# Four kv heads in one 128-partition tile, with a block mask on the attention weights, in a decode attention kernel

## The chip, the cores and the metric

The kernel runs on one core of one Trainium2 chip. The metric is device time in microseconds (us) of one execution. The span in a profile is a little shorter than the time (205.2 us against 207.02 us in the profiled run of the kernel before). Each run is therefore marked fast, slow or, where it stands alone, unknown, and only fast runs are compared.

Engine names in the profile: PE is TensorE (matmuls), PEld its weight loads, DVE is VectorE, ACT is ScalarE, POOL is GpSimd, SP is SyncE, which issues the DMAs here.

## The reference, cut to what matters

```python
# B=8 sequences, one new token each; D=512; 32 query heads, 8 kv heads, head size 128; cache of 8192
def _A_ref(x, k_cache, v_cache, wq, wo):
    W = min(4096, max(256, Sk // 4))                  # 2048: only the last 2048 positions count
    q = (x @ wq).reshape(B, 1, 32, 128) ...
    k = jnp.repeat(k_cache[:, :, Sk - W:, :], 4, axis=1)
    v = jnp.repeat(v_cache[:, :, Sk - W:, :], 4, axis=1)
    p = softmax(einsum("bhqd,bhkd->bhqk", q, k) * 128 ** -0.5)
    return einsum("bhqk,bhkd->bhqd", p, v) ... @ wo

h  = x + _A_ref(layernorm(x), k_cache, v_cache, wq, wo)
out = h + _B_ref(layernorm(h), ...)                   # a small MLP, not touched by the change
```

All data are bfloat16. The caches are 8 sequences x 8 heads x 2048 positions x 128 values, 33.6 MB each for K and V, and every byte is used once. With one token per sequence there is little arithmetic per byte. The natural limit is the rate at which K and V come in (408 GB/s in the profile below).

A word on correctness: with the given inputs attention moves the output very little, so that the comparison with the reference passes even for a kernel whose attention is wrong.

## The kernel before: the parts that matter

A step is one kv head of one sequence, 2048 positions. Its K lies in SBUF as 128 partitions of 16 positions, which is one run of 4 KB per partition in HBM. Sixteen 128x128 transposes turn it into `kT` (head size on partitions, positions along the free axis). Four QK matmuls, one per quarter of the positions, go to four column groups of the array. The query operand `qblk[:, b, g, :]` is zero outside the heads of kv head `g`, so the eight steps of a sequence accumulate into one 128 x 512 score tile in PSUM, whose partitions are 4 quarters x 32 query heads.

```python
e.dma_start(knat[:, ks, :].rearrange("p (c d) -> p c d", c=NC),          # NC = 16: 4 KB per partition
            A_k_cache[b, g, W0:SK, :].rearrange("(p c) d -> p c d", c=NC)).then_inc(sem_k[ks], 16)
...
def pe_T(e, i):                                  # 16 transposes of one step
    ...
    for c in range(NC):
        ins = e.matmul(buf[:, c * 128:(c + 1) * 128], knat[:, ks, c * DH:(c + 1) * DH],
                       ident_b[:, :], is_transpose=True)
...
def pe_QK(e, i):                                 # 4 matmuls of 512 neighbouring columns
    ...
    for q in range(4):
        ins = e.matmul(S_ps[32 * q:32 * (q + 1), b % 2, :], qblk[:, b, g, :],
                       kT_sb[:, i % NKT, 512 * q:512 * (q + 1)],
                       start=(g == 0), stop=(g == G - 1), tile_position=(0, 32 * q), ...)
...
def act_exp(e, b):                               # one exp per sequence, 512 neighbouring values written
    ...
    e.activation(P_sb[:, j, :], S_ps[:, j, :], ACT.Exp, bias=negmcol[:, j:j + 1], scale=1.0,
                 accum_out=lcol[:, j:j + 1]).then_inc(sem_exp, 1)
...
def pe_PT_lrowT(e, b):                           # 4 transposes of P
    ...
def pe_PV(e, b, glist, first, last):             # 128 matmuls of 4 columns per sequence
    ...
            e.matmul(misc[:, ...], vnat[:, vs, c * DH:(c + 1) * DH], pT_sb[:, b % 2, c, R * g:R * (g + 1)], ...)
```

The order of work on TensorE is one software pipeline: the transposes of step p, QK of step p-2, and in the steps after a sequence's last QK its max, exp, P transposes and PV. K has 15 slots of 512 KB, V has 16.

## Time and profile before

| | before |
|---|---|
| time, median of 3 runs | 207.6 us (207.4 to 207.75) |
| span of the profiled run, mean granted clock | 205.2 us, 0.834 |
| busy TensorE / ScalarE / VectorE | 159.2 / 81.4 / 83.5 us |
| DMA rate between 20 and 160 us | 408 GB/s |
| TensorE waiting for K ahead of its transposes | 20.8 us, 22 times |

The first lines are the page's view of the span in 40 slices. Each digit is a tenth of the slice: busy share for PE and DMA, granted clock for PEclk.

```profile
PE   1039975999599967995799878797998698875745
PEclk9999999797979799979995998599859797675557
DMA  6999999999999999999999999999999999999980
GB/s 206 434 398 415 409 407 409 407 411 408 403 410 406 408 410 410 406 406 410 409 410 405 409 411 410 407 406 410 406 409 408 407 410 385 359 394 328 394 334 28
```

DMA is full from the second slice almost to the end, at 403 to 415 GB/s while the caches stream. TensorE has holes, and its clock drops now and then (to about 0.5 in the lowest slices). The chain that ended last, by engine and by line, says the same: 84% of the span hangs on DMA and on the queue that issues it.

```profile
DMA 53%; SPq 31%; PE 13%; issue 2%; DVE 0%
...
```

Then the groups of instructions (line, engine, operation, out<-in, shapes, count | busy us, mean ns | idle before, and what ended most of it):

```profile
L388 PE MATMUL kT_ps<-ident_b,knat 128*128 128x128 bf16 x1024 | 83.8, 248 | 21.7 <-DMA knat<-in_A_k_cache_dram 20.8
L418 PE MATMUL S_ps<-kT_sb,qblk 128*32 128x512 bf16 x256 | 29.0, 440 | 0.0
L439 ACT ACTIVATE P_sb<-S_ps,negmcol 128x512 bf16<-128x512 f32 x8 | 5.5, 687 | 7.7 <-DVE negmcol L431 7.6
```

Nearly all idle time of TensorE ahead of the transposes was ended by a K load: this is a kernel that waits for memory. The exp is done once per sequence and takes 687 ns. Last, some lines of the timeline (start, duration, engine, line), in a stretch at full clock (granted clock 1.00 from 79.0 to 84.3 us):

```profile
81.28 1.07 PE L388 MATMUL kT_ps<-ident_b,knat 128*128 128x128 bf16 x16 [0.47 <-DMA knat<-in_A_k_cache_dram]
82.28 0.40 PE L418 MATMUL S_ps<-kT_sb,qblk 128*32 128x512 bf16 x4
82.61 1.75 PE L526 MATMUL misc<-pT_sb,vnat 128*128 128x4 bf16 x64
```

From start to start, the 16 transposes take 1.00 us and QK 0.33 us. Durations of single lines overlap (81.28 + 1.07 lies after 82.28), and the profile models the ends of matmuls. So I cost by starts. The 16 transposes read 2048 columns in 1.00 us, and the four QK matmuls, one per column group, read 2048 columns in 0.33 us. That agrees with the four column groups running side by side.

### The profile page before, as it was taken

To read this page: it belongs to the slowest core of one execution; us is meant where nothing else is said; L and a number is where in the kernel's file an instruction comes from. 1 tells how busy PE (TensorE), PEld (TensorE's weight loads), DVE (VectorE), ACT (ScalarE), POOL (GpSimd) and SP (SyncE) were. 2 spreads that over 40 slices of the span, in tenths; PEclk is the share of its full clock that TensorE was granted. 3 is DMA by queue.
4 is the path that set the end of the run, shared out by engine and by line. 5 is a ranking of instruction groups with operands and counts; after the bars stand their busy time and mean duration, and the time that the engine had idled before them with its cause. 6 is when DMAs were issued, how large, how long until landed. Compare 5 with 4: busy or idle time off the path is not lost.

```text
span 205.2 us, 6281 instructions
## 1 busy us (share of the span) xinstructions
PE 159.2 (78%) x2744; PEld 122.6 (60%) x2744; DVE 83.5 (41%) x197; ACT 81.4 (40%) x100; POOL 3.0 (1%) x13
## 2 busy tenths in 40 slices
PE   1039975999599967995799878797998698875745
PEld 0039853697469654963487648574876476554632
DVE  5103544544453446343543554346435353352130
ACT  3203656515541554153513551176135431350040
POOL 5000000000000000000000000000000000000000
PEclk9999999797979799979995998599859797675557
DMA  6999999999999999999999999999999999999980
GB/s 206 434 398 415 409 407 409 407 411 408 403 410 406 408 410 410 406 406 410 409 410 405 409 411 410 407 406 410 406 409 408 407 410 385 359 394 328 394 334 28
DMA packets 24266, 79.59 MB, mean 388 GB/s; under 512 B 2200, under 2 KB 6320, under 8 KB 24112
## 3 DMA queue, kind: packets, MB, share of 16 engines
q1 hardware_dynamic: 24224, 79.19, 98.1%
q8 instruction: 22, 0.36, 0.7%
q14 instruction: 4, 0.03, 0.0%
q10 hardware_dynamic: 16, 0.00, 0.0%
HBM read 79.18 MB, written 0.01 MB: 386 GB/s over the span
## 4 chain that ended last, share of the span: by engine, by line
DMA 53%; SPq 31%; PE 13%; issue 2%; DVE 0%
DMA knat<-in_A_k_cache_dram 47%; SPq L239 17%; SPq L249 9%; PE kT_ps L388 6%; DMA knat<-in_B_w_dram 6%; SPq L259 4%; PE misc L526 3%; PE b L692 1%; PE S_ps L418 1%; SPq L277 1%; PE b L507 0%; DVE out_sb L702 0%; SPq L230 0%; SPq L231 0%; PE b L473 0%
## 5 line engine op out<-in xcount | busy, mean ns | idle before, releaser
L388 PE MATMUL kT_ps<-ident_b,knat 128*128 128x128 bf16 x1024 | 83.8, 248 | 21.7 <-DMA knat<-in_A_k_cache_dram 20.8
L399 ACT ACTIVATE kT_sb<-kT_ps 128x1024 bf16<-128x1024 bf16 x64 | 65.4, 1022 | 87.0 <-PE kT_ps L388 87.0
L388 PEld LDWEIGHTS kT_ps<-ident_b,knat 128*128 128x128 bf16 x1024 | 71.8, 113 | 38.6 <-DMA knat<-in_A_k_cache_dram 30.3
L406 DVE COPY kT_sb<-kT_ps 128x1024 bf16<-128x1024 bf16 x64 | 44.2, 691 | 62.8 <-PE kT_ps L388 62.8
L526 PE MATMUL misc<-pT_sb,vnat 128*128 128x4 bf16 x1024 | 29.0, 165 | 3.0 <-issue 1.4
L526 PEld LDWEIGHTS misc<-pT_sb,vnat 128*128 128x128 bf16 x1024 | 27.5, 98 | 6.1 <-issue 3.2
L418 PE MATMUL S_ps<-kT_sb,qblk 128*32 128x512 bf16 x256 | 29.0, 440 | 0.0
L418 PEld LDWEIGHTS S_ps<-kT_sb,qblk 128*32 128x32 bf16 x256 | 6.7, 94 | 9.0 <-issue 3.2
L439 ACT ACTIVATE P_sb<-S_ps,negmcol 128x512 bf16<-128x512 f32 x8 | 5.5, 687 | 7.7 <-DVE negmcol L431 7.6
L360 PE MATMUL S_ps<-xlnT,wbig 128*128 128x8 bf16 x128 | 3.6, 168 | 6.3 <-DMA wbig<-in_A_wq_dram 6.3
L536 DVE TENSOR_TENSOR prod_sb<-misc,w_sb 128x128 f32<-128x128 f32 x8 | 2.3, 292 | 14.6 <-PE misc L526 14.6
L512 DVE COPY w_sb<-b 128x128 f32<-128x128 f32 x8 | 2.3, 292 | 13.2 <-PE b L507 13.2
L360 PEld LDWEIGHTS S_ps<-xlnT,wbig 128*128 128x128 bf16 x128 | 3.5, 104 | 6.4 <-issue 6.4
L429 DVE TENSOR_REDUCE mcol<-S_ps 128x1 f32<-128x512 f32 x8 | 5.5, 682 | 0.6 <-PE S_ps L418 0.6
L584 ACT ACTIVATE std<-var,eps_t 128x8 f32<-128x8 f32 x1 | 0.3, 301 | 12.5 <-DVE var L635 12.5
L376 DVE TENSOR_SCALAR qblk<-S_ps 128x32 bf16<-128x32 f32 x8 | 0.9, 181 | 9.7 <-PE S_ps L360 9.7
L463 ACT ACTIVATE a_row<-d_row 1x128 f32<-1x128 f32 x8 | 2.4, 306 | 5.9 <-DVE d_row L456 5.9
L446 PE MATMUL misc<-ident_f,mcol 128*1 128x128 f32 x16 | 3.8, 328 | 1.0 <-DVE negmcol L431 1.0
L507 PE MATMUL b<-w_row,ones_row 1*128 1x128 f32 x16 | 4.2, 343 | 0.0
L602 PE MATMUL S_ps<-oT_all,wbig 128*128 128x8 bf16 x128 | 3.7, 168 | 0.5 <-DMA wbig<-in_A_wo_dram 0.5
L602 PEld LDWEIGHTS S_ps<-oT_all,wbig 128*128 128x128 bf16 x128 | 3.6, 104 | 0.6 <-DMA wbig<-in_A_wo_dram 0.6
L662 PE MATMUL misc<-uT,knat 128*128 128x8 bf16 x56 | 1.7, 168 | 2.7 <-DMA knat<-in_B_w_dram 2.7
(77 smaller groups left out, 68.6 us busy)
## 6 DMA issues: line engine op xcount, KB each, us to landing
knat<-in_A_k_cache_dram SPq DMA_DIRECT2D x64, 512.0 KB, 15.7
vnat<-in_A_v_cache_dram SPq DMA_DIRECT2D x64, 512.0 KB, 15.8
wbig<-in_A_wq_dram SPq DMA_DIRECT2D x1, 4096.0 KB, 12.2
wbig<-in_A_wo_dram SPq DMA_DIRECT2D x1, 2048.0 KB, 20.3
knat<-in_B_w_dram SPq DMA_DIRECT2D x1, 1792.0 KB, 12.1
wbig<-in_A_wo_dram SPq DMA_DIRECT2D x1, 1024.0 KB, 12.4
wbig<-in_A_wo_dram SPq DMA_DIRECT2D x2, 512.0 KB, 11.2
knat<-in_B_w_dram SPq DMA_DIRECT2D x1, 1024.0 KB, 12.6
```

The lines of the kernel that those rows point to most:

```text
L239: e.dma_start(vnat[:, vs, :].rearrange("p (c d) -> p c d", c=NC), A_v_cache[b, g, W0:SK, :].rearrange("(p c) d -> p c d", c=NC),).then_inc ...
L249: e.dma_start(knat[:, ks, :].rearrange("p (c d) -> p c d", c=NC), A_k_cache[b, g, W0:SK, :].rearrange("(p c) d -> p c d", c=NC),).then_inc ...
L259: e.dma_start(wo_v[:, h0:h1, :], A_wo[h0 * 128:h1 * 128, :].rearrange("(h p) n -> p h n", p=128)).then_inc(sem_wo[j], 16)
L360: ins = e.matmul(S_ps[:, 0, h * B:(h + 1) * B], wq_v[:, kc, h * DH:(h + 1) * DH], xlnT[:, kc * B:(kc + 1) * B], start=(kc == 0), stop=(kc ...
L388: ins = e.matmul(buf[:, c * 128:(c + 1) * 128], knat[:, ks, c * DH:(c + 1) * DH], ident_b[:, :], is_transpose=True)
L399: e.activation(kT_sb[:, i % NKT, 0:W // 2], kT_ps[i % 2][:, 0:W // 2], ACT.Copy).then_inc(sem_Elo, 1)
L406: e.tensor_copy(kT_sb[:, i % NKT, W // 2:W], kT_ps[i % 2][:, W // 2:W]).then_inc(sem_Ehi, 1)
L418: ins = e.matmul(S_ps[32 * q:32 * (q + 1), b % 2, :], qblk[:, b, g, :], kT_sb[:, i % NKT, 512 * q:512 * (q + 1)], start=(g == 0), stop=(g ...
L429: ins = e.tensor_reduce(mcol[:, j:j + 1], S_ps[:, j, :], AX.X, ALU.max)
L439: e.activation(P_sb[:, j, :], S_ps[:, j, :], ACT.Exp, bias=negmcol[:, j:j + 1], scale=1.0, accum_out=lcol[:, j:j + 1]).then_inc(sem_exp, 1)
L526: ins = e.matmul(misc[:, OT4.start + q * H + R * g:OT4.start + q * H + R * (g + 1)], vnat[:, vs, c * DH:(c + 1) * DH], pT_sb[:, b % 2, c, ...
L602: ins = e.matmul(hT_ps[:, k * B:(k + 1) * B], wo_v[:, h, k * 128:(k + 1) * 128], oT_all[:, h, :], start=False, stop=(h == H - 1), skip_gro ...
```

## The change

The intent: make the DMA packets larger. Four kv heads share the 128 partitions, 32 partitions per head, so that a partition's run in HBM is 64 positions, 16 KB in place of 4 KB. One transfer is 2 MB. K, V and the weights share ten slots of 16 KB per partition.

The layout has a price. After a transpose, a column of `kT` belongs to one of four heads, and the columns are in partition order. The change uses that partition order with `GL` as the innermost index (partition = 4 x position block + head, from the `"g (p c) d -> p g (c d)"` source order of the transfer), so the columns of one head are every fourth one:

- QK of one step (a quarter of the positions of four heads) becomes 16 matmuls of 128 columns, each reading every fourth element of `kT`.
- PV takes all four heads of a tile in one matmul of 16 columns. For that, the weights of a position may be non-zero only where the head fits. P becomes a block-masked tile `Pm` of 128 x 2048, made by four exps with a per-partition scale and bias (scale 0 and bias -10000 where the head does not fit, which gives 0), each writing every fourth element.
- P is then transposed by 16 transposes, like a step of K, and copied out of PSUM by the same two engines.
- PV remains 128 matmuls per sequence, in two halves four steps apart.

```diff
+GL = 4
+PP = 128 // GL
+C = W // PP
+NT = 4
+NS = 10
...
+                    src = cache[b, GL * gq:GL * (gq + 1), W0:SK, :].rearrange("g (p c) d -> p g (c d)", c=C)
...
+            kv = kT_sb[:, i % NKT, :].rearrange("q (c s p g) -> q s g c p", s=4, p=PP, g=GL)
             ins = None
-            for q in range(4):
-                ins = e.matmul(S_ps[32 * q:32 * (q + 1), b % 2, :], qblk[:, b, g, :],
-                               kT_sb[:, i % NKT, 512 * q:512 * (q + 1)],
-                               start=(g == 0), stop=(g == G - 1),
-                               tile_position=(0, 32 * q), skip_group_check=True)
+            for gl in range(GL):
+                for q in range(4):
+                    ins = e.matmul(S_ps[32 * q:32 * (q + 1), b % 2, t * 128:(t + 1) * 128],
+                                   qblk[:, b, GL * gq + gl, :], kv[:, q, gl, :, :],
+                                   start=(gq == 0 and t == 0 and gl == 0), stop=(gq == 1 and gl == GL - 1),
+                                   tile_position=(0, 32 * q), skip_group_check=True)
...
-            e.activation(P_sb[:, j, :], S_ps[:, j, :], ACT.Exp, bias=negmcol[:, j:j + 1], scale=1.0,
-                         accum_out=lcol[:, j:j + 1]).then_inc(sem_exp, 1)
+            dst = Pm_sb[:, j, :].rearrange("q (c g) -> q g c", g=GL)
+            ins = None
+            for gl in range(2 * half, 2 * half + 2):
+                ins = e.activation(dst[:, gl, :], S_ps[:, j, :], ACT.Exp, bias=bias4[:, j, gl:gl + 1],
+                                   scale=mask[:, gl:gl + 1], accum_out=lcol4[:, j, gl:gl + 1])
+            ins.then_inc(sem_exp, 1)
...
+            for c in range(C):
+                cc, q = divmod(c, 4)
+                o = OT4.start + q * H + GL * R * gq
+                k0 = cc * 128 + q * H + GL * R * gq
+                ins = e.matmul(misc[:, o:o + GL * R], slots[:, slot, c * DH:(c + 1) * DH],
+                               pT_sb[:, b % 2, k0:k0 + GL * R], ...)
...
```

## The prediction

19.3 us per sequence (batch) at full clock, 21.1 with a quarter of half-clock steps, eight of these from about 18 us on, and a tail of 13.6 us give a span of 201 and a time of 203 us.

> **What bounds the kernel now.** DMA. The page's 40-slice view shows the DMA engines full from slice 2 to 38, at 406 to 411 GB/s while the caches stream. K and V are 67.1 of 79.2 MB, so about 164 us of the 205.2 us span. The chain of waits is 53% DMA plus 31% DMA issue. TensorE is second and close: 159.2 us busy (78%), and only about 21 us of idle before the transposes is put down to K loads. By the timeline, a step of 512 KB (16 transposes + QK) takes 1.33 us at full clock (0.99 + 0.34) and 2.36 us at half clock. A half-clock stretch of about 7 us follows each batch's PV, which is 3.8 us of four-column matmuls. [...] the granted clock falling to 0.50 after PV agrees.

> **What the change removes.** K and V rows go from 4 KB to 16 KB. 4 KB at 408 GB/s is 160.6 ns per packet and engine. The wq load (32 KB rows) ran at about 432 GB/s between 3 and 12.6 us, so a packet costs about 9 to 10 ns beyond its bytes. [...] Estimate for 16 KB: 428 GB/s, so 157 us for K and V: 7.5 us saved. The weights at the end (360 GB/s) are not changed. If DMA alone bound it: about 200 us.

> **What it adds, per batch (8 batches).**
> - TensorE: QK as 16 matmuls of 128 columns in place of 4 of 512: estimate 0.42 us per step against 0.34 (+0.6); 16 P transposes in place of 4 (+0.7). PV stays 128 matmuls (3.5 us), but in two pieces of 1.75 us four steps apart[...].
> - ScalarE: four exps (0.69 us each) in place of one, one more 1.02 us eviction: 81 us busy becomes about 107. Not a bound by itself, but it is in order: max, two exps, an eviction, two exps must pass before the P transposes. I estimate a TensorE stall of 2 us per batch.

> TensorE per batch at full clock: 8 x 1.42 + 1.0 (P) + 3.5 (PV) + 1.4 (small) + 2.0 (stall) = 19.3 us, against 19.6 us of DMA (8.39 MB at 428 GB/s). Each tenth of half-clock steps adds 0.7 us; I expect a quarter: 21.1 us. Then TensorE, not DMA, is the limit: it starts at about 18 us (first 2 MB tile), ends the last PV at about 187, and the tail without DMA waits (13.6 us, from the timeline) gives a span of 201 and a time of 203. Ten slots give some 30 us of slack, so DMA should not stall before the end.

> **Prediction: 203.0 us, 198.5 to 212.** Faster by over 2%: 0.50, within 2%: 0.30, slower by over 2%: 0.20.

> **What would show each step.** Cache-phase GB/s near 428 (wrong if still about 410); busy TensorE gaps before the P transposes released by exp, about 2 us; QK groups of about 0.42 us; K-load waits of TensorE nearly gone; last PV later than the landing of the last V; granted clock 0.85 to 0.9; ScalarE about 107 us.

> **What would make it wrong.** QK that doesn't overlap in the four column groups[...]; a half clock most of the time (slower, 212 and over); heads 2 MB apart in one transfer slowing HBM; or a warm clock throughout (DMA-bound, 199 to 200).

## The result, and the profile after

Ratios here are the mean time of one kernel's fast runs over the mean of the other's fast runs of the same rounds, so not quite the ratio of the medians that are quoted.

| | before | after |
|---|---|---|
| time, median of 4 runs | 207.62 us | 238.73 us (235.38 and 238.5 fast; 238.96 and 239.86 slow) |
| ratio of fast runs | | 1.1414 (95% interval 1.1285 to 1.1543) |
| span, clock (profiled run) | 205.2 us, 0.834 | 233.6 us, 0.866 |
| busy TensorE / ScalarE / VectorE | 159.2 / 81.4 / 83.5 us | 171.9 / 123.5 / 88.2 us |
| DMA packets | 24266 | 10577 |
| DMA rate between 20 and 160 us | 408 GB/s | 425 GB/s |

The kernel is 14% slower. It was predicted 2% faster. The profiled run is one of the fast ones. Its 40 slices:

```profile
PE   1068995699659965997299838993897739917866
PEclk9999999589999957799979997999799788955555
DMA  7999999999999999999999999999999991000000
GB/s 271 426 387 438 421 426 440 410 440 422 415 433 410 438 418 429 424 429 426 426 421 432 421 424 424 419 435 381 369 417 374 349 374 59 3 3 0 3 3 4
```

The memory side did what was asked of it. The rate is up by 4%, and all loads are over in slice 34, at about 195 us, 39 us before the end. The granted clock is no worse than before. TensorE, on the other hand, has deep holes. The chain of what ended last has moved from DMA to the engines:

```profile
PE 62%; ACT 16%; issue 9%; DMA 7%; DVE 5%; SPq 0%; ACTq 0%
PE kT_ps L403 30%; ACT Pm_sb L470 13%; PE S_ps L444 13%; PE misc L556 12%; DMA slots<-in_A_k_cache_dram 7%; ACT kT_sb L423 2%; DVE mcol L456 2%; PE b L531 2%; PE S_ps L638 2%; PE b L728 1%; PE misc L508 1%; PE misc L698 1%; DVE bias L458 1%; DVE kT_sb L428 1%; ACT L470 1%
```

The groups show where. The exps no longer take 687 ns but 1486, QK is 1024 matmuls, and TensorE stands for 29.8 us ahead of the P transposes:

```profile
L403 PE MATMUL kT_ps<-ident_b,slots 128*128 128x128 bf16 x1024 | 76.5, 233 | 6.3 <-issue 5.1
...
L470 ACT ACTIVATE Pm_sb<-S_ps,bias,mask 128x512 bf16<-128x512 f32 x32 | 44.0, 1486 | 14.8 <-DVE bias L458 14.8
L444 PE MATMUL S_ps<-kT_sb,qblk 128*32 128x128 bf16 x1024 | 40.5, 291 | 3.6 <-issue 2.3
L403 PE MATMUL kT_ps<-ident_b,Pm_sb 128*128 128x128 bf16 x128 | 12.8, 278 | 29.8 <-ACT Pm_sb L470 29.8
```

One of the eight stalls on the timeline, as the lines of ScalarE and TensorE around it:

```profile
58.89 0.63 PE L444 MATMUL S_ps<-kT_sb,qblk 128*32 128x128 bf16 x16
...
59.45 1.07 PE L403 MATMUL kT_ps<-ident_b,slots 128*128 128x128 bf16 x16
...
60.58 1.49 ACT L470 ACTIVATE Pm_sb<-S_ps,bias,mask 128x512 bf16<-128x512 f32 x1 [1.00 <-DVE bias L458]
...
61.86 1.49 ACT L470 ACTIVATE Pm_sb<-S_ps,bias,mask 128x512 bf16<-128x512 f32 x1
...
62.63 1.07 PE L403 MATMUL kT_ps<-ident_b,slots 128*128 128x128 bf16 x16
...
63.13 1.07 ACT L423 ACTIVATE kT_sb<-kT_ps 128x1024 bf16<-128x1024 bf16 x1
...
64.09 1.48 ACT L470 ACTIVATE Pm_sb<-S_ps,bias,mask 128x512 bf16<-128x512 f32 x1
...
65.35 1.49 ACT L470 ACTIVATE Pm_sb<-S_ps,bias,mask 128x512 bf16<-128x512 f32 x1
...
66.91 1.07 PE L403 MATMUL kT_ps<-ident_b,Pm_sb 128*128 128x128 bf16 x16 [3.21 <-ACT Pm_sb L470]
```

ScalarE begins an exp every 1.26 us (65.35 - 64.09), with one eviction of K in between, and needs from 60.58 to about 66.8 us for four of them. TensorE can do two steps meanwhile, and then stands. The QK group of this stretch began at 58.89 us and the next transposes at 59.45: 0.56 us for a QK that took 0.33.

The waits of TensorE between 18 and 219 us, longest first (us in total, times, longest), show a third item:

```profile
PE kT_ps L403 <- ACT Pm_sb L470: 29.8, 8, 4.8
PE kT_ps L403 <- issue: 5.1, 4, 2.1
PE S_ps L444 <- issue: 2.3, 1, 2.3
PE misc L556 <- issue: 2.3, 2, 1.5
...
```

"Issue" means that the engine waited for nothing that the profile shows. It adds up to 9.7 us here. The same view of the kernel before, between 17 and 188 us, has 2.1 us of it.

So three candidates explain the excess, and I put a size to each from the traces. TensorE's main loop runs from 18.2 us to 218.5 us, which is 25.0 us per sequence where the prediction had 21.1. The wait for the exps is 29.8 / 8 = 3.7 us per sequence, against 2.0 predicted. QK is 8 x (0.57 - 0.42) = 1.2 us over its estimate (0.57 us is the usual distance from a QK group to the transposes after it). The gaps called issue, 9.7 / 8 = 1.2 us, were not in the prediction at all. Together that is 4.1 us, where 3.9 us are missing. The sizes fit, but their causes are only names so far. Why does an exp take twice as long? Why is QK slower? What are the gaps? And is the DMA side as innocent as it looks?

### The profile page after: what moved, and what is told of

It reads as the page before. It is cut to its first block, busy times and chain, and to the rows that moved or that the text cites. A ratio compares the mean times of both kernels' runs of the same rounds, so it can differ in the third digit from the quotient of the medians.

```text
span 233.6 us, 8015 instructions
## 1 busy us (share of the span) xinstructions
PE 171.9 (74%) x3608; PEld 141.1 (60%) x3608; DVE 88.2 (38%) x208; ACT 123.5 (53%) x157; POOL 3.0 (1%) x13
## 2 busy tenths in 40 slices
DMA packets 10577, 79.69 MB, mean 341 GB/s; under 512 B 672, under 2 KB 4784, under 8 KB 6192
## 4 chain that ended last, share of the span: by engine, by line
PE 62%; ACT 16%; issue 9%; DMA 7%; DVE 5%; SPq 0%; ACTq 0%
PE kT_ps L403 30%; ACT Pm_sb L470 13%; PE S_ps L444 13%; PE misc L556 12%; DMA slots<-in_A_k_cache_dram 7%; ACT kT_sb L423 2%; DVE mcol L456 2%; PE b L531 2%; PE S_ps L638 2%; PE b L728 1%; PE misc L508 1%; PE misc L698 1%; DVE bias L458 1%; DVE kT_sb L428 1%; ACT L470 1%
## 5 line engine op out<-in xcount | busy, mean ns | idle before, releaser
L403 PE MATMUL kT_ps<-ident_b,slots 128*128 128x128 bf16 x1024 | 76.5, 233 | 6.3 <-issue 5.1
L403 PEld LDWEIGHTS kT_ps<-ident_b,slots 128*128 128x128 bf16 x1024 | 64.5, 105 | 20.1 <-issue 18.0
L470 ACT ACTIVATE Pm_sb<-S_ps,bias,mask 128x512 bf16<-128x512 f32 x32 | 44.0, 1486 | 14.8 <-DVE bias L458 14.8
L444 PE MATMUL S_ps<-kT_sb,qblk 128*32 128x128 bf16 x1024 | 40.5, 291 | 3.6 <-issue 2.3
L403 PE MATMUL kT_ps<-ident_b,Pm_sb 128*128 128x128 bf16 x128 | 12.8, 278 | 29.8 <-ACT Pm_sb L470 29.8
L556 PEld LDWEIGHTS misc<-pT_sb,slots 128*128 128x128 bf16 x1024 | 27.0, 97 | 6.9 <-issue 5.8
L556 PE MATMUL misc<-pT_sb,slots 128*128 128x16 bf16 x1024 | 28.6, 170 | 2.9 <-issue 2.3
L403 PEld LDWEIGHTS kT_ps<-ident_b,Pm_sb 128*128 128x128 bf16 x128 | 10.8, 127 | 31.6 <-ACT Pm_sb L470 31.6
L444 PEld LDWEIGHTS S_ps<-kT_sb,qblk 128*32 128x32 bf16 x1024 | 22.2, 107 | 11.2 <-issue 5.9
L470 ACT ACTIVATION_READ_ACCUMULATOR Pm_sb<-S_ps,bias,mask 128x1 f32 x32 | 8.6, 268 | 0.0
## 6 DMA issues: line engine op xcount, KB each, us to landing
slots<-in_A_k_cache_dram SPq DMA_DIRECT2D x16, 2048.0 KB, 31.4
slots<-in_A_v_cache_dram SPq DMA_DIRECT2D x2, 1024.0 KB, 14.2
slots<-in_A_wo_dram SPq DMA_DIRECT2D x1, 1024.0 KB, 12.6
```

What stands on the lines that cost most here:

```text
L403: ins = e.matmul(buf[:, c * 128:(c + 1) * 128], src[:, c * 128:(c + 1) * 128], ident_b[:, :], is_transpose=True)
L444: ins = e.matmul(S_ps[32 * q:32 * (q + 1), b % 2, t * 128:(t + 1) * 128], qblk[:, b, GL * gq + gl, :], kv[:, q, gl, :, :], start=(gq == 0 ...
L470: ins = e.activation(dst[:, gl, :], S_ps[:, j, :], ACT.Exp, bias=bias4[:, j, gl:gl + 1], scale=mask[:, gl:gl + 1], accum_out=lcol4[:, j, g ...
L556: ins = e.matmul(misc[:, o:o + GL * R], slots[:, slot, c * DH:(c + 1) * DH], pT_sb[:, b % 2, k0:k0 + GL * R], start=(c == 0), stop=(cc == ...
```

## The experiments

The theory after the result was: the exps are slow because they write every fourth element (rival: because of their additional scale operand, or something else in the four-exp form), QK is slow because of the number of matmul pairs, and the gaps come with the number of instructions (rival: the large packets hold something back). The DMA part of the prediction is right.

Nine kernels ran. The first four share their runs of the kernel before (median 207.49 us), the next four another set (207.53 us), the last one a third (207.55 us).

### 1. The exp writes runs of 32 neighbours (wrong)

Everything is as in the change, but each exp writes its 512 values as 16 runs of 32 neighbours. The values land in wrong places of `Pm`. The instructions, their operands and their order are the same.

```diff
-            dst = Pm_sb[:, j, :].rearrange("q (c g) -> q g c", g=GL)
+            dst = Pm_sb[:, j, :].rearrange("q (c g p) -> q g c p", g=GL, p=PP)
...
-                ins = e.activation(dst[:, gl, :], S_ps[:, j, :], ACT.Exp, bias=bias4[:, j, gl:gl + 1],
+                ins = e.activation(dst[:, gl, :, :], S_ps[:, j, :].rearrange("q (c p) -> q c p", p=PP), ACT.Exp, bias=bias4[:, j, gl:gl + 1],
```

> The changed kernel, but each exp writes its 512 values in runs of 32 neighbours instead of every fourth element (result wrong on purpose: the heads' columns stand in another order than V's partitions). Theory, the spread-out write makes an exp slow (1486 ns in the trace of the change against 687 ns before): an exp falls to 690 to 800 ns, TensorE's wait for the exps from 29.8 us to 10 to 15 us, and the time from 238 to 216 to 224 us. Rival, the exp is slow for its operands (a scale and a bias read per partition, inputs of -10000): it stays near 1490 ns and the time within 1% of the change.

Measured: 219.69 us, ratio to before 1.0543 (1.0474 to 1.0611). The two groups that matter:

```profile
L470 ACT ACTIVATE Pm_sb<-S_ps,bias,mask 128x512 bf16<-128x512 f32 x32 | 24.6, 778 | 17.1 <-DVE bias L458 17.1
...
L403 PE MATMUL kT_ps<-ident_b,Pm_sb 128*128 128x128 bf16 x128 | 10.2, 243 | 12.7 <-ACT Pm_sb L470 12.7
```

What follows: the exp falls from 1486 to 778 ns, and the wait from 29.8 to 12.7 us. The write of every fourth element cost 708 ns per exp. The rival explains at most the remaining 91 ns over the 687 of the kernel before. In the ratios to before, the gain is 1.1414 - 1.0543, which is 18 us of 207.5. It is the largest single piece. But 11 us to the kernel before remain, and the gaps called issue have grown to 13.8 us in this run.

### 2. QK once per two steps (16 matmuls of 256 columns)

If the number of matmul pairs makes QK slow, half as many of twice the length should be faster. The reading stays at every fourth element.

```diff
-            kv = kT_sb[:, i % NKT, :].rearrange("q (c s p g) -> q s g c p", s=4, p=PP, g=GL)
+            kv = kT_sb[:, i % NKT:i % NKT + 2, :].rearrange("q n (c s p g) -> q s g (n c) p", s=4, p=PP, g=GL)
...
-                    ins = e.matmul(S_ps[32 * q:32 * (q + 1), b % 2, t * 128:(t + 1) * 128],
+                    ins = e.matmul(S_ps[32 * q:32 * (q + 1), b % 2, t * 128:(t + 2) * 128],
```

> The changed kernel, but QK runs once per two steps: 16 matmuls of 256 columns in place of 32 of 128, the same products (result right). Theory, QK is bound by the number of weight-load and matmul pairs (16 in 0.57 us, at both clocks): two steps' QK takes 0.6 to 0.7 us at full clock in place of 1.14, and the time falls by 12 to 17 us, to 221 to 227. Rival, QK is bound by reading columns with a stride of four: 1.1 us per two steps as now, time within 1% of the change.

Measured: 230.19 us, ratio 1.1067 (1.1029 to 1.1106).

```profile
L403 PE MATMUL kT_ps<-ident_b,Pm_sb 128*128 128x128 bf16 x128 | 15.1, 312 | 39.4 <-ACT Pm_sb L470 39.4
...
L444 PE MATMUL S_ps<-kT_sb,qblk 128*32 128x256 bf16 x512 | 35.3, 404 | 0.2 <-issue 0.2
```

What follows: the theory about QK missed. One QK of two steps takes 1.01 us at full clock, against 2 x 0.57, where 0.6 to 0.7 was expected. With this reading pattern QK went with the columns, not with the pairs: half the pairs with the same columns took 1.01 us for 1.14. Yet two other things changed. The gaps called issue are nearly gone (0.2 us for 9.7), with 3096 matmuls in place of 3608. And the wait for the exps grew from 29.8 to 39.4 us: a good part of what TensorE saved was spent waiting, because the exps pace it. This is no clean test of the gaps, since a longer wait elsewhere also hides what would have been a gap.

### 3. The same tiles by packets of 4 KB

Each 2 MB transfer is cut into four transfers whose runs are 4 KB. All the arithmetic stays.

```diff
-                        e.dma_start(dst, src).then_inc(sem_slot[slot], 16)
+                        for r in range(4):
+                            e.dma_start(dst[:, r * CT * DH:(r + 1) * CT * DH],
+                                        src[:, :, r * CT * DH:(r + 1) * CT * DH]).then_inc(sem_slot[slot], 16)
```

> The changed kernel, but each 2 MB tile comes as four DMAs with 4 KB runs (result right): the transfer part of the change undone alone. Theory, DMA does not set the time of the changed kernel: cache-phase rate back to about 408 GB/s, DMA ends about 8 us later, time within 1% of the change. Rival, 16 KB packets hold up TensorE's instruction fetch: the gaps of TensorE that wait for nothing in the trace (9.7 us in the K and V stretch) fall to about 2 us and the time falls by 5 us or more.

Measured: 238.01 us, ratio 1.1467 (1.1435 to 1.1498), at 407 GB/s between 20 and 160 us. The gaps called issue are 8.6 us, the wait for the exps 31.4 us.

What follows: with the rate back at that of the kernel before, the time is that of the change, within the noise. In the change the DMA rate is worth nothing that these runs show. And the gaps do not come from the large packets.

### 4. Packets of 16 KB under the kernel before (wrong)

The other half of the change alone: the kernel before, with 16 slots of K in place of 15, loads four heads per 2 MB transfer in runs of 16 KB, and computes on them as if nothing had changed. Positions and heads are mixed up, so the result is wrong.

```diff
-                    A_k_cache[b, g, W0:SK, :].rearrange("(p c) d -> p c d", c=NC),
+                    A_k_cache[b, 4 * gq:4 * gq + 4, W0:SK, :].rearrange("g (p c) d -> p g (c d)", c=64),
```

> The kernel before, with only the transfers of the change: K and V as 2 MB tiles of four heads in 16 KB runs, the compute as before (result wrong on purpose: rows and heads are mixed). Theory, the predicted gain of the longer rows is real and only the added compute hides it: cache-phase rate about 426 GB/s, time 198 to 202 us. Rival, the compute before cannot follow a faster stream or coarse tiles: rate 426 for a while, but the time stays at 206 or more.

Measured: 202.06 us, ratio 0.9741 (0.9722 to 0.9761), at 426 GB/s between 20 and 160 us.

```profile
GB/s 211 419 426 422 426 436 429 426 419 432 426 427 432 416 422 426 427 429 422 429 426 419 426 429 432 419 432 418 429 419 422 426 420 357 396 365 347 397 218 5
...
L389 PE MATMUL kT_ps<-ident_b,knat 128*128 128x128 bf16 x1024 | 84.2, 249 | 20.4 <-DMA knat<-in_A_k_cache_dram 20.4
```

What follows: the first half of the prediction stands. The larger packets, with the 2 MB transfers and the one more slot that come with them, are worth 5.4 us when the arithmetic is left alone (predicted 7.5, to about 200). All that the change lost, it lost in the arithmetic: from 202 us to 237 us, the mean of its fast runs.

### 5. QK reads neighbours: a permutation in the transposes

A transpose multiplies by the identity. If it multiplies by a permutation instead, the columns of `kT` come out sorted by head at no cost (from start to start the 16 transposes take 1.00 us either way), and QK reads runs of 32 neighbours. The exps still write every fourth element. The result is right.

```diff
+            e.tensor_copy(perm_b[:, :].rearrange("k (g p) -> k g p", g=GL),
+                          ident_b[:, :].rearrange("k (p g) -> k g p", g=GL))
...
-                               ident_b[:, :], is_transpose=True)
+                               (perm_b if kind == "k" else ident_b)[:, :], is_transpose=True)
...
-            kv = kT_sb[:, i % NKT, :].rearrange("q (c s p g) -> q s g c p", s=4, p=PP, g=GL)
+            kv = kT_sb[:, i % NKT, :].rearrange("q (c s g p) -> q s g c p", s=4, p=PP, g=GL)
```

> The changed kernel, but the K transposes multiply by a permutation matrix in place of the identity, so that each head's 32 columns stand side by side in kT_sb and QK reads runs of 32 neighbours instead of every fourth column (16 matmuls of 128 columns per step as in the change; result right). Theory, which the run with paired QK points to (1.01 us per two steps, so the cost went with columns and not with pairs): the spread-out read halves the column rate. QK falls from 0.57 to 0.33 to 0.40 us per step at full clock and the time by 8 to 14 us, to 224 to 230. Rival, 16 weight-load and matmul pairs cost 0.57 us whatever they read: no change.

Measured: 232.65 us, ratio 1.1201 (1.1171 to 1.1231). The timeline at full clock, and the group:

```profile
70.67 0.41 PE L447 MATMUL S_ps<-kT_sb,qblk 128*32 128x128 bf16 x16
71.01 1.07 PE L406 MATMUL kT_ps<-perm_b,slots 128*128 128x128 bf16 x16
...
```

```profile
L447 PE MATMUL S_ps<-kT_sb,qblk 128*32 128x128 bf16 x1024 | 30.1, 244 | 5.5 <-issue 5.4
```

What follows: QK takes 0.34 us per step (71.01 - 70.67), as in the kernel before, with the same 16 pairs that took 0.57. So it was the reading of every fourth element that made QK slow. At half clock there is next to nothing to gain: there QK took 0.57 us with every fourth element (2 groups of the change's trace) and 0.55 with neighbours (3 groups of this one). The gain is small, 4 to 6 us (1.1414 - 1.1201, or 1.1467 - 1.1201 against number 3, whose arithmetic is that of the change and whose interval is narrower), less than expected, although QK's busy time fell by 10.4 us (40.5 to 30.1). The wait for the exps stayed (28.1 us), and the gaps called issue grew from 9.7 to 14.9 us. TensorE became faster, and what it gained went partly into those gaps.

### 6. Sixteen QK matmuls under the kernel before

The counter-test to number 5: the kernel before, with its four matmuls of 512 columns split into sixteen of 128 neighbouring columns. It asks what the pairs cost by themselves. It ran once, so the state of the run is unknown, and its time is only an indication.

```diff
-            for q in range(4):
-                ins = e.matmul(S_ps[32 * q:32 * (q + 1), b % 2, :], qblk[:, b, g, :],
-                               kT_sb[:, i % NKT, 512 * q:512 * (q + 1)],
+            for r in range(4):
+              for q in range(4):
+                ins = e.matmul(S_ps[32 * q:32 * (q + 1), b % 2, 128 * r:128 * (r + 1)], qblk[:, b, g, :],
+                               kT_sb[:, i % NKT, 512 * q + 128 * r:512 * q + 128 * (r + 1)],
```

> The kernel before, with QK cut into 16 matmuls of 128 neighbouring columns per step in place of 4 of 512 (result right): the number of instructions of the change (3608 on TensorE) without its spread-out read. Theory, spread-out read: QK 0.33 to 0.40 us per step at full clock, time within 1% of before. Rival, number of pairs: 0.57 us per step. If the gaps in which TensorE waits for nothing come from the number of instructions, they appear here too (5 us or more in the K and V stretch, against 2.1 before); if they need the change's other parts, they don't.

Measured: 208.63 us in one run (runs of the kernel before beside it: 207.16 to 207.66).

```profile
L419 PE MATMUL S_ps<-kT_sb,qblk 128*32 128x128 bf16 x1024 | 28.7, 237 | 0.4 <-DVE kT_sb L406 0.3
```

```profile
PE kT_ps L388 <- issue: 3.0, 4, 1.6
...
PE misc L527 <- issue: 1.9, 2, 1.5
```

What follows: 28.7 us busy, against 29.0 with four matmuls. The twelve more pairs per step cost the array nothing here. But the gaps called issue are 4.9 us, against 2.1 in the kernel before; I had asked for 5 or more, and this is one run. (The 3608 in the expectation is a slip: the run has 3512 pairs, as P keeps its 4 transposes.) What this run changed is the number of instructions, and nothing about packets, exps or reading patterns.

### 7. One exp, and the masks on VectorE

A right version of number 1: one exp per sequence into a contiguous tile, as before, and two multiplications on VectorE that spread it into `Pm` by a broadcast mask. They write neighbours.

```diff
+            e.activation(P_sb[:, j, :], S_ps[:, j, :], ACT.Exp, bias=negmcol[:, j:j + 1], scale=1.0,
+                         accum_out=lcol[:, j:j + 1]).then_inc(sem_exp, 1)
...
+            p_bc = bass.AP(tensor=p1.tensor, offset=p1.offset, ap=[p1.ap[0], [1, 256], [0, GL]])
+            m_bc = bass.AP(tensor=m1.tensor, offset=m1.offset, ap=[m1.ap[0], [0, 256], [1, GL]])
+            e.tensor_tensor(Pm_sb[:, h * half:h * (half + 1)].rearrange("q (c g) -> q c g", g=GL), p_bc, m_bc,
+                            ALU.mult).then_inc(sem_pm, 1)
```

> The changed kernel, but the exp runs once over 128x512 with neighbouring writes, as before the change, and VectorE makes the four masked copies by two multiplications with a broadcast mask (result right). Theory, the four spread-out exps on ScalarE are what TensorE waits for: exp 690 ns, ScalarE busy falls from 123 to about 87 us, TensorE's wait ahead of the P transposes from 29.8 us to 4 to 12 us, time 212 to 220. Rival, the wait is for the chain as such (max, exp, masks) whoever does it: 25 us or more of wait remain, time over 230.

Measured: 221.9 us, ratio 1.0704 (1.0656 to 1.0753).

```profile
L401 PE MATMUL kT_ps<-ident_b,Pm_sb 128*128 128x128 bf16 x128 | 10.0, 240 | 14.7 <-DVE Pm_sb L476 14.7
...
L476 DVE TENSOR_TENSOR Pm_sb<-P_sb,mask_b 128x1024 bf16<-128x1024 bf16 x16 | 18.7, 1204 | 0.0
```

What follows: 15 us better than the change (1.1414 - 1.0704, times 207.5), a bit less than expected. The wait ahead of the P transposes is 14.7 us. Two masks of 1.20 us, behind one exp, are not much quicker than four exps of 0.78 us. The gaps called issue are 14.2 us.

### 8. All of it, with the P transposes one step later

Numbers 5 and 7 together, and the P transposes and the first half of PV moved back by one step, so that TensorE has another step of K to do while the masks are made. By the sum of the single gains this had to beat the kernel before.

```diff
-                if p == 2 * NT * b + 2 * NT - 1 + LQK + 2:
+                if p == 2 * NT * b + 2 * NT - 1 + LQK + 3:
...   (the edits of numbers 5 and 7)
-                elif p == base + 3:
+                if p == base + 4:
                     PE.append(lambda e, b=b: pe_PV(e, 2 * b))
```

> The changed kernel with all three mends: permuted K transposes, one exp with the masks on VectorE, and the P transposes and first PV one step later (result right). Theory: TensorE per batch at full clock 8 x 1.35 + 1.0 + 3.4 + 1.4 = 16.6 us against 19.7 us of DMA at 426 GB/s, so DMA is the limit again and the time is that of the kernel before with 16 KB runs, 199 to 204 us, faster than before. If something else of the change costs (slots freed late, gaps), it stays above 206.

Measured: 217.15 us (6 runs, one of them slow), ratio 1.045 (1.0428 to 1.0472). That missed by 13 us or more. The profile fell into the slow run (219.42 us, clock 0.85, where the fast runs have 0.857 to 0.864), so I use it for what TensorE waited for, not for its length. Waits of TensorE, 17 to 200 us:

```profile
PE misc L557 <- issue: 7.9, 4, 3.1
PE kT_ps L404 <- issue: 7.3, 4, 2.8
PE kT_ps L404 <- DVE Pm_sb L479: 5.7, 6, 1.6
PE S_ps L445 <- issue: 4.7, 3, 2.3
...
```

What follows: the wait for the masks is down to 5.7 us, as it should be, and the first and the second cause are gone. In their place the gaps called issue are 7.9 + 7.3 + 4.7 = 19.9 us, twice those of the change. Here the third cause had to be named.

The trace records every DMA packet with its queue, and one queue of the page is named "instruction". Its packets are 16,384 bytes each and come all through the run. Their number follows TensorE's program: TensorE executes 5653 instructions in the kernel before (weight loads, matmuls and waits) and 7397 after, and the page counts 22 and 29 packets. That is 257 and 255 instructions per packet. At 256 per packet, numbers 6 and 9 should have 28.1 and 24.8, and their traces have 28 and 25. So I read a packet as 256 instructions of TensorE's program. I laid the gaps called issue beside those packets. In the listing, the first number is the moment at which the gap ended, the second its length, the third the number of TensorE weight-load and matmul pairs executed by then, the fourth the landing of the last instruction packet, and the fifth the time from this landing to the end of the gap (all us, from the records of the traces).

```
after
 38.32  0.67   469   37.05  1.27
 83.58  2.30  1218   82.06  1.52
107.24  1.47  1591  105.73  1.51
130.81  0.83  1964  129.50  1.31
137.23  1.17  2089  135.79  1.44
158.92  1.23  2464  157.50  1.42
181.89  2.07  2838  180.51  1.38
number 8
 36.44  0.99   469   35.15  1.29
 51.41  1.02   717   49.98  1.42
 71.57  1.41  1091   70.19  1.38
 78.17  2.26  1218   76.56  1.61
 98.41  2.29  1591   97.18  1.22
119.97  2.15  1964  118.42  1.55
133.49  0.37  2213  132.01  1.48
147.26  2.83  2464  145.80  1.46
161.46  1.96  2712  160.03  1.43
168.39  1.51  2838  167.12  1.27
189.02  3.06  3212  187.66  1.37
```

The packets also keep a distance. Between 15 and 170 us, while the data stream fills the DMA engines, no two of them started less than 5.9 us apart in any of the kernels. Their mean distance is 8.7 us in the kernel before, 7.5 after, 7.0 here and 6.7 in number 6. After and here a sequence needs 128 transposes of K, 16 of P, 128 QK, 128 PV and 6 small matmuls, 406 pairs or 812 instructions; before it was 596, and in number 2 it is 684 (waits, some 20 per sequence, are not counted). At 256 per packet and 6.3 us per packet (the smallest distance in this kernel), 812 take 20.0 us. That is an estimate, but it is no less than the 19.7 us that 8.39 MB of K and V take at 425 GB/s. By this estimate the instruction packets could bind by themselves, and the gaps show that waits move onto them when the other waits are taken away. The estimate does not account for all of number 8, whose main loop (18.3 to 201.7 us) took 22.9 us per sequence.

### 9. Number 8 with QK once per two steps

If that is right, fewer instructions have to help, even though in number 6 the pairs cost the array nothing (28.7 us busy, against 29.0). Number 8 with the edit of number 2 has 684 instructions per sequence. The result is right.

```diff
-            kv = kT_sb[:, i % NKT, :].rearrange("q (c s g p) -> q s g c p", s=4, p=PP, g=GL)
+            kv = kT_sb[:, i % NKT:i % NKT + 2, :].rearrange("q n (c s g p) -> q s g (n c) p", s=4, p=PP, g=GL)
...
-                    ins = e.matmul(S_ps[32 * q:32 * (q + 1), b % 2, t * 128:(t + 1) * 128],
+                    ins = e.matmul(S_ps[32 * q:32 * (q + 1), b % 2, t * 128:(t + 2) * 128],
```

> The kernel with the three mends (c1_all, 217.15 us) and QK once per two steps in 16 matmuls of 256 neighbouring columns: 3096 matmuls instead of 3608, the same arithmetic (result right). Theory from the DMA records of all runs so far: TensorE's program comes in blocks of 16 KB, 256 instructions, never closer than 6.0 us while the data queue is full; c1_all needs 812 instructions per batch, 3.2 blocks, some 20.6 us, which is more than the 19.7 us of data. Here it is 684, 2.7 blocks, about 17.4 us: the gaps in which TensorE waits for nothing fall from 20 us to under 3, DMA is the limit, time 199 to 204 us, below before by over 2%. Rival, the gaps have another cause (packet size, semaphores, the order of the schedule): they stay over 10 us and the time over 210.

Measured: 202.19 us (201.25 to 203.48), ratio to before 0.9738 (0.9716 to 0.9761). It beats both kernels: the kernel before by 2.6%, 5.4 us of the medians, and the change's fast runs (235.38 and 238.5) by some 35 us.

```profile
DMA 59%; PE 29%; DVE 5%; issue 4%; SPq 2%; ACT 1%; DVEq 0%
...
L404 PE MATMUL kT_ps<-perm_b,slots 128*128 128x128 bf16 x1024 | 73.1, 231 | 23.9 <-DMA slots<-in_A_k_cache_dram 18.4
...
L445 PE MATMUL S_ps<-kT_sb,qblk 128*32 128x256 bf16 x512 | 21.1, 283 | 3.3 <-issue 3.3
```

What follows: the chain is back on DMA, TensorE waits 18.4 us for K, as in the kernel before (20.8), and the time is within 0.2 us of number 4's 202.06, the DMA part alone. The gaps called issue are down from 19.9 to about 6 us, not under 3 as I had expected. In fairness, not all of the 15 us between numbers 8 and 9 is waiting for instruction packets. QK itself became cheaper, from 29.3 to 21.1 us of busy time (from the profile of a slow and of a fast run). The two cannot be separated in this pair. Numbers 2 and 6 do separate them in part: in number 6 QK's own time is unchanged (28.7 and 29.0 us) and the gaps grow with the instructions, and in number 2 they vanish with the instructions, though with the reservation made there.

## Why the prediction was right or wrong

What was right:

- *"What bounds the kernel now. DMA."* Number 4 changed nothing but the transfers and gained 2.6%.
- *"Estimate for 16 KB: 428 GB/s"*: 425 after, 426 in number 4, against 408 GB/s with 4 KB before and 407 in number 3, whose arithmetic is that of the change. The packets' own durations show the step best: the median is 160 ns for 4 KB, 612 for 16 KB and 1220 for the 32 KB of wq. Four packets of 4 KB are 640 ns, 28 ns more than one of 16 KB, or some 9 ns for each of the three packets saved, which is near the prediction's 9 to 10 ns; from 16 to 32 KB it is 4 ns. The prediction's 432 GB/s for wq is close to the 430 of these packets on 16 engines; over its window, 3 to 12.6 us, the profile's view has 387.
- *"If DMA alone bound it: about 200 us"*: 202.06 in number 4. Saved were 5.4 us, not 7.5.
- *"Then TensorE, not DMA, is the limit"*, starting at about 18 us (18.2), the waits for K nearly gone (1.2 us for 20.8), the clock between 0.85 and 0.9 (0.866), and DMA without a stall before the end.
- The clock, in part. In the kernel before, a half-clock stretch began near the end of each of the first seven PVs (3.2 us before it to 0.6 us after it), as the prediction had it, but these stretches were 3.4 or 6.8 us long and not always its 7, and three more (from 35.1, 55.6 and 161.4 us) came without a PV. The granted clock after is at half from 205.0 us on, where the last stall (4.8 us) and the tail follow. What sets the granted clock was not shown. But the clock was not what went wrong.

The step that failed is the sum for TensorE, 21.1 us per sequence, measured 25.0, and in it above all the stall before the P transposes. Three terms of it:

1. *"four exps (0.69 us each)"* and, from that, *"I estimate a TensorE stall of 2 us per batch"*. I took the duration from the exp of the kernel before, which writes neighbours. The exp of the change writes every fourth element and takes 1486 ns (number 1: 778 ns with neighbours). ScalarE was busy 123.5 us, where 107 was predicted, and the stall was 3.7 us on average and up to 4.8. The chain of argument was right (max, two exps, an eviction, two exps, then the P transposes). One duration in it was off by a factor of two. It is worth 15 to 18 us (numbers 7 and 1).
2. *"QK as 16 matmuls of 128 columns ...: estimate 0.42 us per step"*. Measured 0.57. I had looked at the number of matmuls and their length, and not at what they read. With neighbours the same 16 take 0.34 us (numbers 5 and 6), better than my estimate. With every fourth element they take 0.57. It is worth 4 to 6 us of time (number 5).
3. Not in the prediction at all: TensorE's instructions per sequence rose from 596 to 812, and the packets that bring them came no less than 6.3 us apart while the data streamed. In the change the gaps behind these packets were 9.7 us; with the first two causes repaired they were up to 19.9 us, in a slow run, while number 8 lay 9.6 us behind the kernel before. How much of the time the gaps cost by themselves is not measured.

The prediction's list of what would make it wrong named QK, the clock, HBM and a full clock throughout. It was QK to a small part, and none of the other three. Its range ended at 212 us, since all doubts in it were about numbers I had thought of.

The three gains are not additive, and I was wrong about this a second time, in number 8. As I read the traces, each repair shortens what TensorE does between two instruction blocks, and so turns part of its gain into a wait for the next block: the gaps went from 9.7 us to 13.8 (number 1), 14.9 (number 5), 14.2 (number 7) and 19.9 (number 8).

Two things stay open. Why instruction packets do not come closer than 6 us is not known: cutting the data packets to 4 KB (number 3) changed neither the gaps (8.6 us) nor the smallest distance (6.2 us), but I could not run the kernel with the data stream taken away. In the tails of the traces, when the data had landed at about 195 us, they did come closer: 5.0 us in the change (from 199.6 to 204.6) and 3.8 us in number 5 (from 198.0 to 201.9). So 6 us is no fixed limit, and the data stream may have a part in it, whatever the size of its packets. And for QK the share of its busy time that went into new gaps is a reading of one profile, not a controlled result.

## What to carry to other kernels

A new data layout can change the access pattern of the engines that touch the data, and here their times with it (an exp from 778 to 1486 ns, QK from 0.34 to 0.57 us per step). Before a duration is carried over from an old profile, check that the new instruction reads and writes in the same pattern, not just the same number of elements; and look for a free place to restore neighbours, such as a permutation in a transpose that is done anyway (1.00 us with it and without it in number 5). Count the instructions of the busiest engine too: when its gaps have no cause in the profile, lay them beside the instruction packets (every gap laid beside them here ended 1.2 to 1.6 us after one). And after each repair, ask which wait will take over.
